# Output projections ahead of the first MLP2 product in five groups, with the PSUM banks handed on in another order

## The chip, the cores and the metric

The kernel runs on one core of one Trainium2 chip. The time is that of one execution on the device in microseconds; a run's time is the median of several executions. Beside it there is one profiled execution, from which all single durations are taken.

## The reference

One transformer block over 2048 tokens of width D = 576: a layer norm, attention in 32 heads of 18 over a dilated window, an output projection with a residual, two layer norms in a row, and an MLP of width 4608 with a residual.

```python
def _A_ref(x, wqkv, wo):
    W, dil = 8, 2
    q, k, v = ...                       # x @ wqkv, split into 32 heads of 18
    idx = pos[:, None] - off[None, :]   # keys at 0, 2, ..., 14 tokens back
    logits = jnp.einsum("bhsd,bhswd->bhsw", q, kg) * scale
    attn = _softmax(jnp.where(mask, logits, -1e9), axis=-1)
    o = jnp.einsum("bhsw,bhswd->bhsd", attn, vg)
    return ... @ wo

def _B_ref(x, w1, b1, w2, b2):
    y = _layernorm(x, axis=-1)
    h = _gelu(jnp.einsum("bsd,df->bsf", y, w1) + b1)
    return jnp.einsum("bsf,fd->bsd", h, w2) + b2

x = A_x
h = x + _A_ref(_layernorm(x, axis=-1), A_wqkv, A_wo)
h2 = h + _B_ref(_layernorm(h, axis=-1), B_w1, B_b1, B_w2, B_b2)
```

## The kernel before

The tokens are cut into 16 tiles of 128, and these are taken in eight groups of two (`GROUPS`). A first stage computes Q, K and V for all tiles. Then the loop at line 985 runs over the groups. While the MLP of one group runs on TensorE (PE), VectorE (DVE) computes attention and ScalarE (ACT) the layer norm (LN2) of the groups that follow. In the loop, `c` and `d` are the two tiles of the next group, `e` and `f` those of the group after it. The whole order on PE, ACT, DVE, SP and POOL is written out by hand: the kernel stands in a manual schedule for all five engines, so each engine executes in the order of the calls.

Groups are counted from 1 in the text, so groups 3 to 8 are `k` = 2 to 7.

**MLP1** (`mlp1`, `mlp1_duo`, matmuls at L217) goes in four visits over nine units of PSUM: the tags p, q; r, s; p, q; r, s, p. A tag is a pair of PSUM banks; there are four tags A to D[...]. After each unit, four GELU activations on ACT (L560) bring it to `h_all` in SBUF. The matmuls use half of the rows of the array each, in two phases; a no-op on POOL marks the end of a first phase.

**MLP2** of groups 3 to 8 (`mlp2_fast`, matmuls at L667) is a seven-product scheme in place of eight block products: products 1 to 7 over `rows` pairs of row blocks, and plain products "11", "12", "21", "22" for the remainder (`rows` is 8, 12, 12, 16, 18, 18 in groups 3 to 8). Five banks hold the results: a and f are the two banks of one tag (`af`), b is in a second tag, bank 7 in a third and bank 5 in a fourth. Some results are needed in two sums. So ACT copies one bank to another (L739) as a start value for further accumulation: step "b" copies a to b after product 1, step "d" b to bank 5 after product 6, step "f" bank 5 to f after product 5. Products 1 and 2 add up in bank a, products 6 and 4 in bank b.

The steps of `mlp2_fast` are a list; a pair such as `(1, all_)` is a product with its rows, a string is another step:

- "wo": the two output projections of the next group's tiles c and d (`wo_visit`, `wo_duo`; `pw` in the profile, 36 matmuls of half the array's rows), in the tags that are bank 7's and bank 5's afterwards. They need `oT`, the attention output transposed by DMA (L433).
- "h" in groups 3 to 6: `ln2_stats(c, d)`, for each tile one addition on DVE that reads the projection (`ln2_h`, L461), then five instructions on ACT (`ln2_act`: L478 and L479 with a read of the accumulator each, and L480) and a power on POOL (L481), and then two DMAs of the bias row (`put_b2`, L505). Sums of `h_all` blocks for the products follow on DVE (`h_sums`, L647). In group 7, "h" takes tile d's statistics to DVE, and it also holds `ln2_send(c)`: two ACT instructions (L486, L175) that need the power on POOL, and a store.
- "e" names bank 7 and bank 5 (`take`). "rest", "o1" and "o0" are additions on DVE that read finished banks and store the output.
- "6" and "7" carry `ln2_send` of c and d in groups 3 to 6 (and attention work on DVE).

```python
for step in steps:
    if isinstance(step, tuple):
        product(step[0], bank[step[0]], *step[1])
    elif step in seed:
        nc.scalar.copy(out=bank[seed[step][1]], in_=bank[seed[step][0]])
    else:
        call([does[step]] if step in does else hooks.get(step, ()))
```

At the end of each group the tags p, q, r, s are renamed for the next one.

## Time and profile before

| | |
|---|---|
| time, median of 3 runs | 365.16 us (365.06 to 365.8) |
| the profiled execution's own time | 365.13 us |
| its span, first to last instruction | 363.3 us |
| PE busy | 357.6 us |
| DVE busy | 300.6 us |
| ACT busy | 228.9 us |
| one MLP1 of two tiles on PE (L217, `pm`) | 17.79 us |
| two output projections (`pw`, 36 matmuls) | 2.31 us |
| product 1 (L667) with 8, 12, 16 rows | 1.09, 1.58, 2.07 us |
| one copy between banks (L739) | 0.38 us |

The busy time of an engine is the union of its instructions. Span and time differ by what lies around the instructions (1.8 us). PE's matmuls overlap, so the ends of single ones say less than the distance between starts. In the timelines, times are in us from the start of the span.

### The profile page before, as it was taken

Reading aid. Unit: us, or ns where it says so; the run is one execution under the profiler, and the core shown is the slowest. Engines: PE = TensorE matmul, PEld = TensorE weight load, DVE = VectorE, ACT = ScalarE, POOL = GpSimd, SP = SyncE. Lnnn points to the kernel's source line nnn. Section 1 sums busy time; section 2 is a strip of 40 time slices with the busy share of each in tenths; the row PEclk is TensorE's granted clock in tenths of the full one; section 3 lists DMA queues with packets and bytes.
Section 4 is the critical chain, followed back from the end, with each engine's and each line's share of the span. In section 5 each row is a group of like instructions: output and inputs, shape, how many; then the busy total and the mean of one; then the engine's idle time right before and its main releaser. Section 6 shows DMA issues by size and latency. Waiting matters only on the chain.

```text
span 363.3 us, 11427 instructions
## 1 busy us (share of the span) xinstructions
PE 357.6 (98%) x4895; PEld 290.5 (80%) x4895; DVE 300.6 (83%) x426; ACT 228.9 (63%) x507; POOL 39.4 (11%) x47
## 2 busy tenths in 40 slices
PE   8999999999999999999999999999999999999996
PEld 4688877888788877887788778877887788778874
DVE  5999999999999999999999899979998498720431
ACT  4779856799526763668556855685568656615630
POOL 2251004000120030103100211020101010100000
PEclk9999999999999999999999999999999999999999
DMA  7989899964445733720552145304530352030001
GB/s 235 299 204 306 223 260 236 363 219 78 145 89 107 218 111 87 152 40 34 137 106 71 35 125 115 72 32 109 118 71 33 74 102 56 3 89 19 2 2 33
DMA packets 61908, 43.70 MB, mean 120 GB/s; under 512 B 31889, under 2 KB 60177, under 8 KB 61857
## 3 DMA queue, kind: packets, MB, share of 16 engines
q1 hardware_dynamic: 59968, 41.13, 41.1%
q0 software_dynamic: 1728, 1.77, 4.8%
q8 instruction: 38, 0.62, 0.7%
q10 hardware_dynamic: 160, 0.07, 0.1%
q14 instruction: 14, 0.11, 0.1%
HBM read 21.10 MB, written 12.42 MB: 92 GB/s over the span
## 4 chain that ended last, share of the span: by engine, by line
PE 94%; DMA 2%; ACT 1%; SPq 1%; DVE 0%; issue 0%
PE pm L217 39%; PE po L667 25%; PE pq L217 14%; PE po L579 10%; PE pw L217 5%; DMA wq_sb<-in_A_wqkv_dram 1%; SPq L104 1%; PE xt_pt L182 1%; DMA x_all<-b_bc 1%; ACT hn L175 0%; ACT hn L479 0%; PE h_pt L182 0%; PE o_pt L182 0%; DVE h L461 0%; ACT hn L478 0%
## 5 line engine op out<-in xcount | busy, mean ns | idle before, releaser
L560 ACT ACTIVATE h_all<-pm,b_sb 128x256 f16<-128x256 f32 (+1 forms) x288 | 108.3, 496 | 74.3 <-PE pm L217 74.3
L217 PE MATMUL pm<-hnT,w_sb 64*128 64x256 bf16 x2304 | 143.0, 269 | 0.0
L217 PEld LDWEIGHTS <-w_sb 64*128 64x128 bf16 x2304 | 111.6, 94 | 15.1 <-issue 1.7
L667 PEld LDWEIGHTS <-h_all 128*128 128x128 f16 x528 | 50.8, 98 | 14.9 <-issue 2.5
L217 PE MATMUL pq<-wq_sb,xnT 64*128 64x288 bf16 x768 | 54.5, 283 | 0.8 <-DMA wq_sb<-in_A_wqkv_dram 0.7
L217 PEld LDWEIGHTS <-xnT 64*128 64x128 bf16 x864 | 42.4, 94 | 11.3 <-issue 1.1
L351 DVE TENSOR_TENSOR prod<-prod 128x2304 bf16<-128x2304 bf16 (+1 forms) x64 | 44.2, 691 | 2.1
L667 PE MATMUL po<-w2a_sb,h_all 128*128 128x288 bf16 (+1 forms) x302 | 42.0, 286 | 0.0
L397 DVE TENSOR_TENSOR prod<-kv_ring,probs 128x4608 bf16<-128x4608 bf16 x16 | 40.9, 2554 | 0.8 <-DMA kv_ring<-kv_dram 0.5
L345 DVE TENSOR_TENSOR prod<-kv_ring,q_all 128x4608 bf16<-128x4608 bf16 x16 | 40.8, 2549 | 0.2
L217 PE MATMUL pm<-hnT,w1h_sb 64*128 64x256 bf16 x288 | 39.2, 269 | 0.0
L403 DVE TENSOR_TENSOR prod<-prod 128x2304 bf16<-128x2304 bf16 (+1 forms) x32 | 33.8, 1057 | 1.0
L579 PEld LDWEIGHTS <-h_all 128*128 128x128 bf16 x288 | 27.8, 98 | 7.9 <-issue 1.0
L481 POOL TENSOR_TENSOR ln_rstd<-ln_var,mhalf 128x1 f32<-128x1 f32 x13 | 14.5, 1115 | 175.1 <-ACT ln_var L480 175.1
L667 PEld LDWEIGHTS <-kv_ring 128*128 128x128 f16 x240 | 23.5, 98 | 6.4 <-issue 0.5
L579 PE MATMUL po<-w2a_sb,h_all 128*128 128x288 bf16 x224 | 28.5, 286 | 0.0
L647 DVE TENSOR_TENSOR kv_ring<-h_all 128x1536 f16<-128x1536 f16 (+3 forms) x10 | 6.9, 687 | 17.3 <-ACT h_all L560 17.3
L667 PE MATMUL po<-w2b_sb,h_all 128*128 128x288 bf16 (+1 forms) x142 | 21.2, 286 | 0.0
L217 PE MATMUL pw<-wo_sb,oT 64*128 64x288 bf16 x256 | 19.5, 283 | 0.0
L162 POOL TENSOR_TENSOR ln_rstd<-ln_veps,mhalf 128x1 f32<-128x1 f32 (+2 forms) x14 | 13.3, 954 | 48.2 <-DVE ln_veps L156 31.8
L217 PEld LDWEIGHTS <-oT 64*128 64x128 bf16 x288 | 13.5, 94 | 4.8 <-issue 1.7
L739 ACT COPY po<-po 128x288 f32<-128x288 f32 x18 | 6.9, 384 | 16.2 <-PE po L667 13.0
(117 smaller groups left out, 383.1 us busy)
## 6 DMA issues: line engine op xcount, KB each, us to landing
w_sb<-in_B_w_dram SPq DMA_DIRECT2D x6, 768.0 KB, 5.5
kv_ring<-kv_dram SPq DMA_DIRECT2D x28, 144.0 KB, 2.6
w2a_sb<-in_B_w_dram SPq DMA_DIRECT2D x4, 1008.0 KB, 6.6
kv_dram<-kv_ring SPq DMA_DIRECT2D x13, 288.0 KB, 3.3
out_dram<-o_sb SPq DMA_DIRECT2D x15, 144.0 KB, 2.5
td<-q_all SPq DMA_DIRECT2D x14, 144.0 KB, 2.2
td<-hn SPq DMA_DIRECT2D x14, 144.0 KB, 1.8
x_all<-in_A_x_dram SPq DMA_DIRECT2D x12, 144.0 KB, 2.9
```

Of the source, the lines that this page charges most:

```text
L162: nc.gpsimd.tensor_tensor(out=rstd[:], in0=veps[:], in1=mhalf[:].to_broadcast([P, n]), op=ALU.pow)
L217: last = nc.tensor.matmul(duo["g"][r ^ swap][i], lhsT=lhsT, rhs=rhs, start=(swap == 0 and i == 0 and kt == 0), stop=(swap == 1 and kt == K ...
L345: nc.vector.tensor_tensor(out=prod[:], in0=k_ring[j % 2], in1=q_all[:, j, :].unsqueeze(1) .to_broadcast([P, W, D]), op=ALU.mult)
L351: nc.vector.tensor_tensor(out=prod[:, :, o * H:o * H + n], in0=prod[:, :, a * H:a * H + n], in1=prod[:, :, c * H:c * H + n], op=ALU.add)
L397: nc.vector.tensor_tensor(out=prod[:].rearrange("p w (d h) -> p w d h", h=H), in0=v_ring[j % 2].rearrange("p w (d h) -> p w d h", h=H), in ...
L403: nc.vector.tensor_tensor(out=prod[:, 0:n, :], in0=prod[:, 0:n, :], in1=prod[:, n:2 * n, :], op=ALU.add)
L481: nc.gpsimd.tensor_tensor(out=rstd[:], in0=var[:], in1=mhalf[:], op=ALU.pow)
L560: pace[0] = nc.scalar.activation(out=hT(grp)[:, f, 0:N], in_=ps[:, r, i * N:(i + 1) * N], func=ACT.Gelu_apprx_tanh, bias=b1_sb[:, f:f + 1] ...
L579: nc.tensor.matmul(banks[half], lhsT=hT(grp)[:, f, i * P:(i + 1) * P], rhs=w2_rows(f)[:, half * HALF:(half + 1) * HALF], start=(f == 0), s ...
L647: nc.vector.tensor_tensor(out=s_slot(t, m0, m1), in0=a, in1=b, op=alu)
L667: nc.tensor.matmul(bank, lhsT=l, rhs=r, start=start, stop=stop, skip_group_check=True)
L739: nc.scalar.copy(out=bank[seed[step][1]], in_=bank[seed[step][0]])
```

## The change

In groups 3 to 7 (those with a next group) the projections "wo" and the step "h" move from behind product 1 to the front of the list of steps, so that they stand directly behind MLP1. In group 7, product 1 also loses its split into two parts. The copy "b" keeps its place behind product 1, and therefore comes after "h". The tags are handed on in another order: the projections are in q and r, product 1 in s and b in p, where before they were in r and s, in q and in p. For the next group the tags are again named in the order bank 7's, bank 5's, b's, af's. Group 8 has no projection; its steps and its tags are as before. No instruction is added or removed.

```diff
     def mlp2_fast(g, rows, tags, wo, hooks):
-        p, q, r, s = tags
         last = wo is None
+        q, p, r, s = tags
         j0, j1 = g
         af = psum_pair(q, "po")
...
         if SR < rows < NM:
-            steps = [(1, all_), "b", "wo", "h", "e", (2, all_), "11", (6, lo), (7, lo), "6", "7", (6, hi), "d", (7, hi), "rest", "in",
+            steps = ["wo", "h", (1, all_), "b", "e", (2, all_), "11", (6, lo), (7, lo), "6", "7", (6, hi), "d", (7, hi), "rest", "in",
                      (5, all_), "f", "exp", (4, all_), "21", "22", "o1", "4", (3, all_), "12", "o0", "3"]
         elif rows <= SR:
-            steps = [(1, all_), "b", "wo", "h", "e", (2, all_), "11", (6, all_), "d", "6", "7", (7, all_), "rest", "in",
+            steps = ["wo", "h", (1, all_), "b", "e", (2, all_), "11", (6, all_), "d", "6", "7", (7, all_), "rest", "in",
                      (5, all_), "f", "exp", (4, all_), "21", "22", "o1", "4", (3, all_), "12", "o0", "3"]
         elif not last:
-            steps = [(1, lo), "wo", (1, hi), "b", "h", "e", (7, lo), (6, all_), "d", "6", "7", (2, all_), (7, hi), "rest", "in",
+            steps = ["wo", "h", (1, all_), "b", "e", (7, lo), (6, all_), "d", "6", "7", (2, all_), (7, hi), "rest", "in",
                      (5, all_), "f", (4, all_), "o1", (3, all_), "o0"]
...
             mlp1(g, mlp1_plan(p, q, r, s, (r, s, p)), m1, mid)
-            mlp2_fast(g, rows, (p, q, r, s), wo, x)
-            p, q, r, s = r, s, p, q
+            mlp2_fast(g, rows, (s, p, q, r) if wo else (q, p, r, s), wo, x)
+            p, q, r, s = q, r, p, s
```

## The prediction

> **What bounds the kernel now.** I read the page's busy shares first, then the chain of waits in order of time, then the timelines of PE, ACT and DVE around the five places that the diff touches.

> ```profile
> PE 357.6 (98%) x4895; PEld 290.5 (80%) x4895; DVE 300.6 (83%) x426; ACT 228.9 (63%) x507; POOL 39.4 (11%) x47
> PE 94%; DMA 2%; ACT 1%; SPq 1%; DVE 0%; issue 0%
> ```

> TensorE is busy for 357.6 of 363.3 us, so nothing but a shorter PE program, or the last few us of idle time, can make the kernel faster. The list of all waits has four rows of PE itself, 2.2 us together; three of them lie before 10 us, the fourth in group 6 (columns: total, times, longest):

> ```profile
> PE po L667 <- ACT po L739: 0.3, 1, 0.3
> ```

> So in the stage of the change PE has 0.3 us to gain, and everything else must come from PE waiting more. The chain in order of time shows what PE does in group 4 (columns: start, length, what):

> ```profile
> 181.44 17.79 PE pm L217 x324
> 199.23 1.58 PE po L667 x12
> 200.80 2.31 PE pw L217 x36
> 203.12 14.81 PE po L667 x120
> ```

> MLP1 (pm), product 1 (po x12), the two output projections (pw x36), and product 2 with the rest (po x120), without a gap. ACT in the same place (start, length, line, operation, idle before):

> ```profile
> 197.52 4.48 ACT L560 ACTIVATE h_all<-pm,b_sb 128x256 f16<-128x256 f32 x12 [2.00 <-PE pm L217]
> 202.03 0.38 ACT L739 COPY po<-po 128x288 f32<-128x288 f32 x1
> 203.46 0.68 ACT L478 ACTIVATE hn<-h 128x576 bf16<-128x576 f32 x1 [1.04 <-DVE h L461]
> ...
> 207.06 0.29 ACT L480 ACTIVATE ln_var<-ln_var,eps 128x1 f32<-128x1 f32 x1
> 207.67 0.38 ACT L739 COPY po<-po 128x288 f32<-128x288 f32 x1 [0.32 <-PE po L667]
> ```

> The last twelve GELUs run until 2.8 us after MLP1. Then the copy "b" (L739, bank a to bank b) at 202.03, while PE is inside the projections: product 2, which accumulates into bank a and so must wait until that copy has read it, starts at 203.05 and never sees it. The ten LN2 instructions of the two tiles follow (3.89 us from 203.46 to the next slot), and then the copy "d".

> [...] "d" of group 6 is held behind the LN2 instructions, its 0.3 us above is the PE wait. [...] L478 measured 677, and I use the rows. [...] The trace shows that a slow state exists: the warm-up matmuls of 512 columns start about 0.42 us apart, 1.2 columns per ns, against 288 columns in 0.123 us later (2.3 per ns), though the granted clock reads 1.0. [...]

> **The change part by part.** It adds and removes no instruction, byte or DMA. Between MLP1's end T and product 2 (in group 7: product 6) PE does the same work in another order, so the time at which PE is ready stays the same. The question is when the copy "b" lets it go on.

> *Projections at T.* Free of cost: their banks are the old q, read by the GELUs of MLP1's third visit long before, and r, whose four GELUs end 1.49 us into the ACT burst, at T - 0.14 in group 3; the second projection starts at T + 0.61. The transposed attention output is there: the latest, group 7's, is issued at 305.87 and takes 2.9 us, landing at 308.8; it is wanted at 308.57 + 0.61 = 309.2, where it now has over 1.5 us more. The two POOL markers keep their place, POOL being idle.

> *Product 1 at T + 2.31.* Its bank is now s, whose GELUs end at T + 1.36. No wait. The other bank turns are equal: the next MLP1 again gets bank 7's, bank 5's, b's and af's buffers, in this order.

> *LN2 earlier.* L461 on DVE (two, 1.42 us) waited until 1.93 us after the first projection matmul; product 1 no longer stands before it (8 rows 1.1, 12 rows 1.6, 16 rows 2.1 us). It comes earlier only as far as DVE and ACT are free: DVE is busy to 165.49, 201.6 and 275.1 in groups 3, 4 and 6. Nothing on PE waited for LN2, so the gain is nothing but group 6's 0.3 us. Its two copies of the bias row on SP and two powers on POOL move with it; both queues are idle there.

> *The copy "b" behind LN2: the cost.* Its place in ACT's program is now behind "h", with the ten LN2 instructions. PE finishes product 1 and stands; all further PE work is queued behind product 2, and DVE's outputs wait with it. Product 2's release = start of L478, + 3.89 us of LN2 (the row spacing above; 3.81 in group 6), + 0.38 copy, + 0.06 to PE (group 6: copy end 283.28, matmul 283.34).
> - Group 3: DVE is held by weight sums until 165.49 as before, so LN2 starts at 166.28 as before, the copy takes the slot of today's "d" at 170.20, PE goes on at 170.64 instead of 165.58: **5.06**.
> - Group 4: L461 at 201.60, L478 0.79 later at 202.39, release 206.72 instead of 203.05: **3.67**.
> - Group 5: h is ready at 238.37, but the GELUs hold ACT until 238.52; release 242.85 instead of 239.53: **3.32**.
> - Group 6: L461 at 275.1, L478 at 275.9, release 280.17 instead of 276.51, **3.66**; less 0.30 as "d" is no longer late: **3.36**.
> - Group 7: "h" also holds the send of tile c (L486, L175), which waits for a power on POOL. Partial sums keep DVE until 311.55, so L478 starts at 312.35, 1.40 before today's 313.75, and the chain moves by that: the end of L175 lets today's "d" start at 317.81, the new "b" at 316.41. The product of 12 rows in bank 7 still covers 1.5 us; product 6 starts at 316.85 instead of 314.68: **2.17**.

> Sum 17.58. Does it come back? DVE's last output add waits for PE's end of a group and starts 0.0 to 0.8 us after it (2.5 in group 6), so the late PE takes DVE with it, and DVE is as late for the next LN2 as now. After group 3 the load is PE's alone again. I take nothing back. The profiled execution took 365.13 us for a span of 363.3; it becomes 382.7, and on the median 365.16, 0.03 above it, **382.8 us**.

> *Bounds.* If DVE were early everywhere, LN2 would start when the GELUs end: 3.8 + 3.3 + 3.3 + 2.5 + 1.2 = 14.1, or 379.3. For the unseen cost of cold matmuls: nothing[...] A gain from a gap is excluded, as PE is the bound. I take nothing, and keep 5.1 for the upper end.

> **The rivals.**
> 1. *The clock falls too.* [...] For it: the slow start. [...]
> 2. *"b" does not queue behind LN2*, if ACT's order differs from the listed one: PE then waits only for the end of product 1, the copy and the release, 0.63 us (in group 4 product 6's stream ends at 207.47, and "d" would release at 208.1), in four groups; group 7's is covered. 365.16 + 2.5 - 0.3 = 367.4. Against: all five engines are in a manual schedule, and today's order on ACT is exactly the listed one.
> 3. *Half is hidden:* DVE delivers tile c earlier and tile d's part overlaps; some 1.9 us less in each of five groups, 373. Against: ten ACT instructions in one queue.
> 4. *The other side, not slower:* the earlier LN2 is what counts, at the group 6 wait, worth 0.3 us, 364.9. It decides only where the bubble before product 2 is under 0.06 us in each group; the copy alone is 0.38. That the order does not change at all would look alike.

> **How the numbers follow.** Chances: the forecast 0.52, rival 1 0.38, rival 2 0.04, rival 3 0.04, rival 4 0.02. Forecast: 382.8. Range: from 380.5, some way to the early-DVE bound, to 388[...]; this leaves out rivals 2 to 4 and some of the rest, less than 2 in 10. A measurement of this kernel tells about 0.2% (0.7 us) from no change: faster 0.01, same 0.02, slower 0.97.

> **What would show it.** Right: a row of waits of PE (L667) on ACT (L739), five times, 17 us together, the longest in group 3 and near 5 us, the shortest in group 7 near 2; on ACT, in groups 3 to 6, L739 directly behind the second L480; pw directly behind pm in the chain, product 1 behind pw; PE's busy time near 357.6 still. A busy time some us higher, with matmul spacing above 0.2 us behind a gap, shows rival 1. Wrong: no such wait, or waits of 0.6 us; or PE waiting for pw's bank, for oT or for DVE instead.

## The result, and the profile after

The changed kernel takes 388.58 us (median of 6 runs, 387.1 to 390.28) against 365.28 us (6 runs beside it): a ratio of 1.0639, with a 95% interval of 1.0599 to 1.0678. The profiled execution took 389.78 us for a span of 388.0, 24.7 us more than the span before. The forecast was 382.8 us with a range to 388.0: direction and most of the size were right; the median lies 0.6 us above the range, with three of the six runs inside it.

The page after, with the busy times, the granted clock of PE in 40 slices, and the chain by engine:

```profile
PE 366.0 (94%) x4895; PEld 294.8 (76%) x4895; DVE 301.1 (78%) x426; ACT 229.0 (59%) x507; POOL 39.1 (10%) x47
...
PEclk9999999999999999969999699989998999999999
...
PE 57%; DVE 26%; ACT 8%; DMA 3%; issue 3%; POOL 1%; SPq 1%; DVEq 0%; POOLq 0%
```

PE executes the same 4895 matmuls, but is busy for 8.4 us longer. The clock row, all 9 before, has four dips. The chain that ended last is no longer PE's alone.

The list of waits of PE (total, times, longest):

```profile
PE po L667 <- ACT po L739: 17.1, 5, 4.7
```

Five waits for a copy between banks, one in each changed group; before there was one of 0.3 us. Group 4 shows what happens. First PE's timeline, from the end of the projections on, then ACT's (start, length, line, operation, idle before):

```profile
207.34 1.14 PE L217 MATMUL pw<-wo_sb,oT 64*128 64x288 bf16 x16
208.41 1.65 PE L667 MATMUL po<-w2a_sb,h_all 128*128 128x288 bf16 x12
213.48 4.00 PE L667 MATMUL po<-w2a_sb,h_all 128*128 128x288 bf16 x16 [3.42 <-ACT po L739]
```

```profile
209.23 0.69 ACT L478 ACTIVATE hn<-h 128x576 bf16<-128x576 f32 x1 [0.38 <-DVE h L461]
...
212.84 0.29 ACT L480 ACTIVATE ln_var<-ln_var,eps 128x1 f32<-128x1 f32 x1
213.04 0.39 ACT L739 COPY po<-po 128x288 f32<-128x288 f32 x1
```

The copy b stands directly behind the second L480. PE resumes 0.05 us after it, at 213.48. And then it is slow: 16 matmuls of product 2 take 4.00 us, 0.24 us from one to the next. In the kernel before, the same 16 took 2.13 us, 0.123 us from one to the next, and PE had not waited:

```profile
203.05 2.13 PE L667 MATMUL po<-w2a_sb,h_all 128*128 128x288 bf16 x16
```

The same place after the change in stretches of time (length, then busy time and count of PE, PEld, DVE, ACT and POOL, granted clock, DMA share, GB/s):

```profile
212.41:213.48 1.07, 0.00 (x0) 0.00 (x0) 1.07 (x2) 0.99 (x4) 0.20 (x1) 0.50 0.00 0
213.48:219.23 5.75, 5.75 (x25) 3.52 (x25) 4.81 (x7) 0.00 (x0) 1.86 (x1) 0.50 0.00 0
219.23:222.00 2.77, 2.77 (x24) 2.23 (x23) 0.00 (x0) 1.08 (x3) 0.00 (x0) 1.00 0.02 6
```

The clock falls to one half at 212.40, within the wait, and returns at 219.23, so that 5.75 us of PE's time run at half speed.

The two costs by group. Standing still is the time from the last matmul's start ahead of the wait, plus 0.1225 us for that matmul (the distance between two starts of L667 at clock 1.00; a single one lasts 0.286 us by the trace before), to the start of the waiting product; the loss is half of the time at clock 0.50 in which PE works, as two starts are 0.24 us apart there.

| group | PE stood still, forecast (us) | measured | time worked at half clock | loss by it |
|---|---|---|---|---|
| 3 | 5.06 | 4.91 | 4.71 | 2.36 |
| 4 | 3.67 | 3.59 | 5.75 | 2.87 |
| 5 | 3.32 | 3.30 | 3.41 | 1.71 |
| 6 | 3.66 | 3.98 | 2.89 | 1.44 |
| 7 | 2.17 | 2.09 | 0 | 0 |
| sum | 17.88 | 17.87 | 16.76 | 8.38 |

17.9 + 8.4 is 26.3. Take off 0.45 for the copy d of group 6, which is no longer late (0.45 by the measure of the table, 0.3 in the list of waits), 1.05 for five saved pairs of a change of matmul kind (shown below), and 0.14 by which this execution already was ahead at the first changed place. Add 0.2 for group 4, where the second projection waited for its transposed input. That makes 24.8, within 0.1 of the 24.7 us.

The runs of the changed kernel spread more than those of the kernel before: three took 387.1 to 387.4 us with a mean clock of 0.982, three 389.8 to 390.3 with 0.973 or 0.974. The second cost fits this. Estimated from the mean clocks, the slower three spent some 20 us at half clock ((1 - 0.974) x 388.0 x 2; the profiled one shows 20.5) and the faster three some 14 ((1 - 0.982) x 385.6 x 2).

### The profile page after: what moved, and what is told of

It reads as the page before. It is cut to its first block, busy times and chain, and to the rows that moved or that the text cites. A ratio compares the mean times of both kernels' runs of the same rounds, so it can differ in the third digit from the quotient of the medians.

```text
span 388.0 us, 11422 instructions
## 1 busy us (share of the span) xinstructions
PE 366.0 (94%) x4895; PEld 294.8 (76%) x4895; DVE 301.1 (78%) x426; ACT 229.0 (59%) x507; POOL 39.1 (10%) x47
## 3 DMA queue, kind: packets, MB, share of 16 engines
q1 hardware_dynamic: 59968, 41.13, 39.4%
## 4 chain that ended last, share of the span: by engine, by line
PE 57%; DVE 26%; ACT 8%; DMA 3%; issue 3%; POOL 1%; SPq 1%; DVEq 0%; POOLq 0%
PE po L667 23%; PE pm L217 17%; PE pq L217 13%; DVE prod L397 5%; DVE prod L351 4%; DVE prod L345 4%; DVE prod L403 4%; ACT hn L479 2%; ACT h_all L560 2%; ACT hn L478 2%; PE po L579 1%; DMA wq_sb<-in_A_wqkv_dram 1%; PE pw L217 1%; DVE h L461 1%; DMA x_all<-b_bc 1%
## 5 line engine op out<-in xcount | busy, mean ns | idle before, releaser
L560 ACT ACTIVATE h_all<-pm,b_sb 128x256 f16<-128x256 f32 (+1 forms) x288 | 108.5, 497 | 75.3 <-PE pm L217 75.3
L217 PE MATMUL pm<-hnT,w_sb 64*128 64x256 bf16 x2304 | 143.0, 269 | 0.0
L217 PEld LDWEIGHTS <-w_sb 64*128 64x128 bf16 x2304 | 111.8, 94 | 14.9 <-issue 1.7
L667 PEld LDWEIGHTS <-h_all 128*128 128x128 f16 x528 | 54.5, 104 | 34.5 <-issue 17.3
L667 PE MATMUL po<-w2a_sb,h_all 128*128 128x288 bf16 (+1 forms) x302 | 48.4, 315 | 15.1 <-ACT po L739 15.1
L217 PE MATMUL pq<-wq_sb,xnT 64*128 64x288 bf16 x768 | 54.5, 283 | 0.6 <-DMA wq_sb<-in_A_wqkv_dram 0.6
L217 PEld LDWEIGHTS <-xnT 64*128 64x128 bf16 x864 | 42.3, 94 | 11.1 <-issue 0.8
L217 PE MATMUL pm<-hnT,w1h_sb 64*128 64x256 bf16 x288 | 39.2, 269 | 0.0
L739 ACT COPY po<-po 128x288 f32<-128x288 f32 x18 | 6.9, 386 | 43.0 <-PE po L667 41.9
L667 PEld LDWEIGHTS <-kv_ring 128*128 128x128 f16 x240 | 23.5, 98 | 8.3 <-issue 2.3
L667 PE MATMUL po<-w2b_sb,h_all 128*128 128x288 bf16 (+1 forms) x142 | 22.8, 301 | 0.0
L217 PE MATMUL pw<-wo_sb,oT 64*128 64x288 bf16 x256 | 19.5, 283 | 0.0
L508 POOL DMA_DIRECT2D x_all<-h x12 | 10.9, 1060 | 73.8 <-DMA x_all<-in_A_x_dram 15.4
(117 smaller groups left out, 387.4 us busy)
```

Source lines behind the costliest of these rows:

```text
L217: last = nc.tensor.matmul(duo["g"][r ^ swap][i], lhsT=lhsT, rhs=rhs, start=(swap == 0 and i == 0 and kt == 0), stop=(swap == 1 and kt == K ...
L508: ins = nc.gpsimd.dma_start(out=x_of(j), in_=h_of.pop(j)[:], accum_op=ALU.add).ins
L560: pace[0] = nc.scalar.activation(out=hT(grp)[:, f, 0:N], in_=ps[:, r, i * N:(i + 1) * N], func=ACT.Gelu_apprx_tanh, bias=b1_sb[:, f:f + 1] ...
L667: nc.tensor.matmul(bank, lhsT=l, rhs=r, start=start, stop=stop, skip_group_check=True)
```

## The experiments

My theory after the result: the copy b behind LN2 is the whole cause of the waiting, and the idle time itself then brings the clock down: it fell at 168.03, 212.40 and 297.74 inside the waits of groups 3, 4 and 6, and at 256.78, 0.93 us behind that of group 5. The main rival: the early projections or the new banks cost something of their own. All kernels were timed beside the kernel before. Diffs are against the changed kernel unless another is named.

**Only the copy put back ahead of LN2**, in each of the three lists:

```diff
-            steps = ["wo", "h", (1, all_), "b", "e",
+            steps = ["wo", (1, all_), "b", "h", "e",
```

> The changed kernel with one thing undone: the copy b stands ahead of h on ACT again, directly behind product 1; projections first and the new bank order stay. Theory (the time is lost because b queues behind LN2 on ACT): PE waits only for the end of product 1, the copy and the release, some 0.6 us in groups 3 to 6 and nothing in group 7, about 2.5 us together, and the clock does not fall; 366.5 to 368 us. Rival (the place of the projections or the new bank order is what costs): waits of 2 us and more stay, 375 us or more.

Measured: 366.84 us, ratio 1.0040 (1.0026 to 1.0054), clock 1.0. PE's wait for the copy:

```profile
PE po L667 <- ACT po L739: 2.1, 4, 0.5
```

One step in ACT's order takes away some 22 of the 23 us, although the early projections and new banks remain. In group 7, where product 7 covers the copy, the time from the start of its MLP1 to that of group 8 is 35.54 us, against 35.75 before: 0.21 us less for the same matmuls.

**The opposite: only the copy moved, in the kernel before.**

```diff
-            steps = [(1, all_), "b", "wo", "h", "e",
+            steps = [(1, all_), "wo", "h", "b", "e",
...
-            steps = [(1, lo), "wo", (1, hi), "b", "h", "e",
+            steps = [(1, lo), "wo", (1, hi), "h", "b", "e",
```

> The kernel before with b moved behind h on ACT and nothing else: product 1, the projections, the banks as before. Theory (the place of b in ACT's order is the whole cause): LN2 starts where it starts now, so the waits are longer than in the changed kernel: 5.1, 4.7, 4.8, 4.7 in groups 3 to 6 and 2.7 in group 7, 22 us, and the clock falls in groups 3 to 6 for 7 to 11 us more; 393 to 398 us. Rival (projections first or the banks are needed for the loss): 365 to 370.

Measured: 397.09 us, ratio 1.0882 (1.0854 to 1.0911), mean clock 0.965 in the profiled execution.

```profile
PE po L667 <- ACT po L739: 21.0, 5, 4.8
```

As expected, and worse than the change itself: with old places and old banks the loss is all there. The early projections even give a part of it back, since LN2 then starts earlier. The rival falls. One thing was not expected: the clock fell in group 7 too, at 344.89, at the end of a wait of only 2.32 us.

**LN2 of one tile ahead of the copy, that of the other behind it.**

```diff
-            steps = ["wo", "h", (1, all_), "b", "e",
+            steps = ["wo", "h", (1, all_), "b", "h2", "e",
...
-                    x["h"] = [c_(ln2_stats, c, d)] + x["h"]
+                    x["h"] = [c_(ln2_h, c), c_(ln2_act, c), c_(ln2_h, d)]
+                    x["h2"] = [c_(ln2_act, d), c_(put_b2, c), c_(put_b2, d)] + x["h2"]
```

> The changed kernel with b put between the LN2 of the two tiles (in group 7 ahead of the send of c). Theory (every ACT instruction ahead of b counts): 1.9 us less of waiting in groups 3 to 6, so about 3.0, 1.7, 1.4 and 2.0, and nothing in group 7, 8 us in place of 17.9; the clock falls in group 3 at most[...]; 370 to 373 us. Rival (a fixed cost of any release through ACT): waits as in the changed kernel less at most 1 us each, 383 us or more.

Measured: 374.01 us, ratio 1.0230 (1.0216 to 1.0244), clock 0.995.

```profile
PE po L667 <- ACT po L739: 7.6, 4, 2.9
```

The waits are as expected: the ACT instructions ahead of the copy count. The time is 1 us above the expected range. The clock fell once, in group 3, at 167.53, though PE waited for only 2.86 us there. In all kept traces the stretches at half clock, up to the last matmul, are 3.41 us long or twice that (in the changed kernel 168.03 to 174.86, 212.40 to 219.23, 256.78 to 260.19 and 297.74 to 301.15). So I sort the idle time by windows of 3.41 us that end at the falls; the choice is mine, made from these lengths. The one that ended at that moment:

```profile
164.12:167.53 3.41, 1.22 (x12) 0.80 (x9) 3.38 (x5) 2.36 (x6) 0.00 (x0) 1.00 0.12 43
```

PE was busy for 1.22 of 3.41 us, so it was 64% idle, and at the end of this window the clock fell to 0.50.

**Matmuls to fill the gap.** They write to the second bank of b's tag, which nobody reads.

```diff
-            steps = ["wo", "h", (1, all_), "b", "e",
+            steps = ["wo", "h", (1, all_), "b", "fill", "e",
...
+        def fill():
+            for _ in range({8: 37, 12: 25, 16: 30, NM: 0}[rows]):
+                mm(bp[:, 1, 0:HALF], h_block(0, 0, 0, 1), w2_block(0, 0, 0, 1), True, True)
```

> The changed kernel with extra matmuls of 288 columns behind product 1 (37, 25, 25, 30 in groups 3 to 6, none in group 7) into a PSUM bank that nobody reads, so that PE is busy while product 2 waits for b. They add work that the result doesn't use. Theory (two costs: about 17.9 us of waiting, and 8.4 us of half rate that follows from the idle time itself): the wait for b ends at the same point of each group, the granted clock stays at 1.0, the time falls by about 8 us, to 380 to 382. Rival (the half rate has another cause than idle time): clock stays near 0.974 and the time near 388.6. Rival (the half rate is only in the records): clock 1.0, time 388.6.

Measured: 403.76 us, ratio 1.1045 (1.1029 to 1.1062), clock 0.979. A miss of the experiment, which decides nothing between the theories: the filler stands behind b in the list and uses the same tag, and it ran behind the copy too (PE's next matmul after product 1 of group 3 starts at 170.46, after 4.68 us of waiting for the copy). It filled nothing and added its own 117 x 0.1225 = 14.3 us. The next kernel lists it ahead of b, in fewer matmuls:

```diff
-            steps = ["wo", "h", (1, all_), "b", "e",
+            steps = ["wo", "h", (1, all_), "fill", "b", "e",
...
+            n = {8: 33, 12: 23 if hooks["k"] == 3 else 21, 16: 25, NM: 0}[rows]
```

> The changed kernel with extra matmuls of 288 columns between product 1 and the copy b in the program (33, 23, 21, 25 in groups 3 to 6, none in group 7), into the unread second bank of b's tag, so many that they end before ACT reaches the copy. They add work that the result doesn't use, all of it inside the time in which PE stands. Theory (about 17.9 us of waiting, and 8.4 us of half rate that follows from the idle time): the wait shrinks to some 0.6 us in each of groups 3 to 6, product 2 starts as long after MLP1 as before, the granted clock stays at 1.0, and the time falls by about 8 us from 388.6, to 380 to 382. Rival (the half rate has another cause than idle time): clock near 0.974, time near 388.6. Rival (the half rate is only in the records): clock 1.0, time 388.6.

Measured: 382.91 us, ratio 1.0484 (1.0469 to 1.0499). The page's clock row:

```profile
PEclk9999999999999999999999999999999999999999
```

PE in group 3, from product 1 with its filler on:

```profile
164.71 5.20 PE L667 MATMUL po<-w2a_sb,h_all 128*128 128x288 bf16 x41
170.64 2.61 PE L667 MATMUL po<-w2a_sb,h_all 128*128 128x288 bf16 x20 [0.73 <-ACT po L746]
```

Product 2 starts 5.93 us after product 1 (5.90 in the changed kernel), but its 20 matmuls take 2.61 us and not 4.90. The changed kernel's line for the same product:

```profile
170.15 4.90 PE L667 MATMUL po<-w2a_sb,h_all 128*128 128x288 bf16 x20 [4.74 <-ACT po L739]
```

More work made the kernel 5.7 us faster, with the mean clock of the profiled execution at 1.0 instead of 0.974: the half clock is real time, and with the idle time filled it did not occur. The time is 0.9 us above what was expected, and 5.7 is not the whole 8.4, in part because three of the six runs of the changed kernel lost less. The two profiled executions differ by 6.9 us (389.78 and 382.87). Of the rest, 0.46 us is that the filled kernel's execution came later to product 1 of group 3, and 0.96 that its product 2 follows product 1 later over groups 3 to 6; 0.7 of this is in group 6, where PE now comes earlier and DVE does not by as much. Together that is about 8.

**How much idle time it takes.** The same kernel with less filler.

```diff
-            n = {8: 33, 12: 23 if hooks["k"] == 3 else 21, 16: 25, NM: 0}[rows]
+            n = {8: 24, 12: 14 if hooks["k"] == 3 else 12, 16: 16, NM: 0}[rows]
```

> As the kernel with the early filler, with 9 matmuls less in each of groups 3 to 6 (24, 14, 12, 16), so that PE is idle for some 1.7 to 2.5 us of each gap instead of 0.6 to 1.5. The filler adds work that the result doesn't use. Theory (a window of 3.4 us that is idle for about two thirds lowers the clock, one that is half idle does not): no fall, or one in group 6 at most; 382.5 to 385. Rival (any gap over 1 us can lower it): clock under 0.98, 387 or more. The waiting is the same for both.

Measured: 383.34 us, ratio 1.0494 (1.0478 to 1.0510). The profiled execution has waits of PE of 1.66 to 1.95 us in groups 3 to 5 and of 3.21 in group 6, and no fall in any. The wait of group 6 lies across two windows, which are 56% and 38% idle:

```profile
288.13:291.54 3.41, 1.50 (x13) 1.06 (x11) 3.34 (x6) 2.96 (x8) 0.75 (x1) 1.00 0.25 89
291.54:294.95 3.41, 2.11 (x18) 1.69 (x18) 2.48 (x7) 3.31 (x8) 0.55 (x1) 1.00 0.06 20
```

One of the four runs took 388.89 us at a mean clock of 0.986. It has no trace, so where the clock fell in it, and why, stays open; that this kernel never loses the clock is not shown. With still less filler:

```diff
+            n = {8: 16, 12: 6 if hooks["k"] == 3 else 4, 16: 8, NM: 0}[rows]
```

> As the kernel with the early filler, with 17 matmuls less in each of groups 3 to 6 (16, 6, 4, 8), so that PE is idle for some 2.7 to 3.5 us of each gap, mostly less than one whole window of 3.4 us. The filler adds work that the result doesn't use. Theory (a window idle for about two thirds is enough): the clock falls in two to four of the groups, mean 0.975 to 0.99, 385 to 390 us. Rival (only a wholly idle window lowers it[...]): no fall but perhaps in group 6, 382.5 to 384.5.

Measured: 389.19 us, ratio 1.0652 (1.0637 to 1.0667). The clock fell in groups 3, 5 and 6 (at 170.72, 252.64 and 297.01), not in group 4. The falls are 24 and 13 times 3.413 us apart, so the windows can be laid through groups 4 (first two rows) and 5:

```profile
208.27:211.68 3.41, 1.97 (x17) 1.43 (x15) 3.41 (x5) 2.93 (x9) 0.62 (x1) 1.00 0.25 89
211.68:215.10 3.42, 1.97 (x17) 1.57 (x17) 3.38 (x3) 1.36 (x4) 2.06 (x1) 1.00 0.03 5
249.23:252.64 3.41, 0.82 (x7) 0.51 (x6) 3.38 (x4) 3.28 (x10) 0.75 (x1) 1.00 0.24 87
```

In group 4 the idle time is split between two windows, each 42% idle: no fall. In group 5 it lies in one, 76% idle, and the clock is down from its end on. In this kernel group 6 waits for 5.3 us, as DVE came later still against PE. Its window is wholly idle, so its fall decides nothing, and the kernel's time says less than the falls of groups 3 (87% idle) and 5.

Laid out in the same way, the windows at full clock in all kept traces fall into two kinds: each one that was 63% idle or more was followed by a fall, and none that was 60% idle or less. The two nearest to the border are group 4 of the kernel before with the late copy, where the clock fell, and group 7 of the first covered version below, where it did not:

```profile
208.36:211.77 3.41, 1.27 (x22) 0.88 (x17) 2.59 (x4) 1.90 (x6) 0.00 (x0) 1.00 0.13 45
291.01:294.42 3.41, 1.37 (x26) 1.40 (x28) 3.41 (x3) 0.00 (x0) 0.89 (x2) 1.00 0.49 120
```

**The banks alone.** New tags, old steps:

```diff
-            steps = ["wo", "h", (1, all_), "b", "e",
+            steps = [(1, all_), "b", "wo", "h", "e",
```

> The kernel before with the new bank order alone: product 1 in s, b in p, projections in q and r, steps in the old order. Theory (the banks cost nothing where the projections come first, but are needed for that): product 1 now follows MLP1 directly in a bank whose GELUs end 1.36 us after MLP1, so PE waits some 1.4 us in each of five groups, about 7 us, 371 to 373 us, no fall of the clock. Rival (bank order is free in any step order): 365.3.

Measured: 372.53 us, ratio 1.0195 (1.0181 to 1.0209).

```profile
PE po L667 <- ACT h_all L560: 6.9, 5, 1.4
```

Five waits for the GELUs that free bank s, 1.4 us each at most, as expected. And the other way round, the projections and the copy early as in the first experiment, but in the old banks:

```diff
-            mlp2_fast(g, rows, (s, p, q, r) if wo else (q, p, r, s), wo, x)
-            p, q, r, s = q, r, p, s
+            mlp2_fast(g, rows, (q, p, r, s), wo, x)
+            p, q, r, s = r, s, p, q
```

> Projections directly behind MLP1 and product 1, b, h behind them, but with the banks of the kernel before (projections in r and s, product 1 in q). Theory (the bank order matters only through the GELUs that free a bank): the second projection is wanted 0.61 us after MLP1 and s is free at 1.36, so PE waits some 0.7 us more in each of five groups than with the new banks: 3.7 us above 366.8, 370 to 371. Rival (bank order is free here): 366.8.

Measured: 371.45 us, ratio 1.0168 (1.0154 to 1.0181), 4.6 us above the same steps with the new banks and 0.45 above the expected range.

```profile
PE pw L217 <- ACT h_all L560: 3.3, 5, 0.7
PE po L667 <- ACT po L739: 2.1, 4, 0.5
```

The new bank order is the right one for the new place of the projections, and no wait of the changed kernel comes from it.

**A version that keeps the early projections and covers the copy.** In groups 5 to 7, products 7 and 6 come behind b; groups 3 and 4 are as before. For group 5, and for group 6:

```diff
+            steps = ["wo", (1, all_), "b", "h", "e", (7, all_), (6, all_), "d", (2, all_), "11", "6", "7", "rest", "in",
...
+            steps = ["wo", (1, all_), "b", "h", "e", (7, lo), (6, lo), (2, all_), "11", (6, hi), "d", (7, hi), "6", "7", "rest", "in",
```

> A version meant to be faster than both: in groups 5, 6 and 7 projections first with the new banks, then product 1, b, h, and products 7 and 6 ahead of product 2, so that PE has other work while b is copied; in group 6 the sends of LN2 behind d; groups 3 and 4 as in the kernel before. Theory: no wait for b in groups 5 to 7, the wait for d in group 6 gone but for 0.1, and 0.2 us less in each of the three groups, as PE changes once less between matmuls on half the rows and on all of them (35.54 us from the start of MLP1 of group 7 to that of group 8 with the copy first, 35.75 before): 0.8 us faster than before, 364.3 to 365.0. Rival (product 7 or 6 waits for DVE's sums or for the projection's bank instead): 365.4 or more, with a wait of PE on DVE in the list.

Measured: 368.30 us, ratio 1.0076 (1.0060 to 1.0091): slower by 3 us, where a gain was expected. No wait for b or d is left, but a new one stands ahead of group 7's MLP1:

```profile
PE pm L217 <- DVE prod L397: 2.7, 1, 2.7
```

The transposes that bring that MLP1's input, from the answer on its tile (count, durations in ns, first and last start):

```profile
L496 SPq DMA_TRANSPOSE hnT<-td x2: 1210/1216/1222, 288.8 to 290.1; - x2
```

The two landed 2.9 us after their issue by the same answer, the second so at 293.0, and PE starts at 293.05. The DVE instruction that the list names is only the one that ended last before; the input is what fits. I had moved the sends of group 6 behind d, and they were needed early: in the kernel before, the last transpose is issued at 287.0 and lands 0.9 us ahead of need. With the sends in their old place in group 6:

```diff
-            ... "11", (6, hi), "d", (7, hi), "6", "7", "rest", "in",
+            ... "11", "6", "7", (6, hi), "d", (7, hi), "rest", "in",
```

> The covered version e6 with one step put back: in group 6 the two sends of LN2 stand ahead of the last rows of product 6 and of d again, as before. Theory (e6 lost 2.7 us only because the later sends brought the transposed input of group 7 to 293.0, while PE wanted it at 290.3): that wait is gone, d is late by 0.3 again, and groups 5, 6 and 7 keep their 0.2 us each; 364.5 to 365.1 us, about 0.5 below the kernel before. Rival (product 7 ahead of product 2 makes DVE or the banks late): a wait of PE of over 1 us stays, 366 us or more.

Measured: 364.75 us, ratio 0.9989 (0.9981 to 0.9998), against 365.17. The 2.7 us are gone. The interval just excludes 1, but 0.1% is less than the 0.2% that I took as what can be told from no change. So the early projections are worth at most some tenths of a us once the copy is covered.

## Why the prediction was wrong in size and right in kind

- **The waiting was right, group by group.** 17.88 us were forecast and 17.87 measured; group 6 was off most, by 0.3. That product 2 stands behind the copy, the copy behind ten instructions of LN2, and where DVE and ACT let LN2 start, all read from the profile before, held. That the sums agree so closely is luck in part: "the time at which PE is ready stays the same" left out the 0.21 us a group for the saved change of matmul kind, and the copy let PE go on some 0.8 us earlier in sum than forecast, counted from the end of MLP1. The early filler takes 382.91 us where 382.8 was forecast (365.16 and 17.58 make 382.74); there the saved 1.05 us and a later product 2, by 0.96, nearly cancel.
- **The failed step is the price of the clock: "I take nothing, and keep 5.1 for the upper end."** The clock fell in four groups, PE worked for 16.76 us at half of it, and this cost 8.4 us; with the early filler no fall was left. The zero and the 5.1 us were the author's estimate: the profile before has no fall up to the last matmul and shows no price for one. In the changed kernel the windows that ended at the falls were 77%, 69%, 73% and 96% idle (groups 3 to 6); over all traces the least idle window with a fall at its end was 63% idle, the most idle one without 60%. In groups 3 and 4, where PE came back in the course of the first 3.41 us, the clock stayed down for 6.83 us, and the loss was 2.36 and 2.87; in groups 5 and 6 it stayed down for 3.41 us, and the loss was 1.71 and 1.44.
- **Rival 1 was the right one**, with 0.38. The range's upper end left 5.1 us for it, and the four falls cost 8.4. Group 7's wait of 1.9 us brought no fall.
- **"I take nothing back" was nearly right.** "The late PE takes DVE with it" held in the changed kernel, where the addition that LN2 needs begins 0.95 us after the last projection matmul of group 6. It did not hold in the fillers, where PE comes to group 6 earlier and DVE does not by as much: 1.65 us in the early filler, 3.41 in the weakest.
- **"The transposed attention output is there"** failed in group 4 alone, by 0.2 us; the prediction had checked group 7's as the latest.
- **"Nothing on PE waited for LN2"** was true but close: the covered version showed that group 7's input comes only 0.9 us early. An earlier LN2 gains nothing there, a later one soon costs.
- The signs came true: five waits of L667 on L739, 17.1 us in the list, from 4.7 in group 3 to 1.9 in group 7; L739 behind the second L480; and busy time up by 8.4 us with 0.24 us between matmuls, the sign named for rival 1.

## What to carry to other kernels

When a step moves ahead of another, look at everything that it puts in the order of each engine: here 2.3 us of PE work moved, and with it 3.9 us of ACT work passed a copy of 0.38 us on which PE depends. Price an idle gap of TensorE with what follows it: in the changed kernel the clock fell to 0.50 for 3.41 or 6.83 us in or just behind waits of 3.1 to 4.7 us, and this cost 1.4 to 2.9 us more for each. A gap that can't be avoided is better short or filled: filled, this kernel took 382.91 us instead of 388.58. One that fell across two windows, each 42% idle (group 4 with the least filler), was spared the second cost, but that came by chance here.
